# A gated attention kernel on one core: longer rows for the opening weights, four gated chunks per bank, and output rows stored over the gate

## The chip, the cores and the metric

The kernel runs on one core of a Trainium2 chip. The metric is the device time of one execution in microseconds (us). Before the change it was 932.59 us, the median of 3 runs (932.0 to 933.07). The span in a profile is 1.7 to 1.9 us shorter than the device time of the same run. A run's time moves by some 0.5 us and at times more from one execution to the next (nine runs of the kernel before spread over 1.0, 1.4 and 0.6 us in the three sets of the experiments), and this study is about differences of about that size, so the text says each time how many runs a number rests on.

## The reference

```python
xn = layernorm(x)                                   # x: 2048 x 640, bf16
q  = xn @ wq                                        # 32 heads of 192
p  = softmax(q @ k[last 512 keys].T * 192 ** -0.5)
s  = (p @ v[last 512 keys]) @ wo
h  = sigmoid(xn @ w_gate) * (xn @ w_up)             # 1536 features
g  = silu(h @ w_down)
out = x + s * g
```

## The kernel before: the parts that matter here

The kernel has three stages: the gate (the lines of `h` and `g`, up to about 166 us), then eight groups of four heads, and within the last group the final sums and the stores. TensorE does matmuls into four double banks of PSUM (`bank[0..3]`), ScalarE the sigmoids, the exponentials and some copies out of PSUM, VectorE most of the rest; GpSimd has a small part in the sums.

The opening. The rows of the weights are cut into pieces, so that work can start before everything is in. `load_f(w, r, f0, f1)` loads columns `f0*128` to `f1*128` of all 640 rows. Two chunks of 128 bf16 are 512 bytes of a row, four are 1 KB.

```python
load_x(0, 1)                                   # one tile of 128 rows of x, 160 KB
load_f(nc.sync, wg_sb, wg_r, 0, 2)             # 320 KB in rows of 512 B
load_x(1, 1)
load_f(nc.sync, wu_sb, wu_r, 0, 2)
load_x(2, 1)
load_f(nc.sync, wg_sb, wg_r, 2, 4)
load_f(nc.sync, wu_sb, wu_r, 2, 4)
load_x(3, 1)
for f0, f1 in ((4, 8), (8, NF)):               # 640 KB each, rows of 1 KB
    load_f(nc.sync, wg_sb, wg_r, f0, f1)
    load_f(nc.sync, wu_sb, wu_r, f0, f1)
```

The first 512 rows of x are four tiles. Each is normalised on VectorE, turned (transposed) by five matmuls of TensorE, and copied out of PSUM. Only then can its matmuls run. For the first four chunks of features this is done tile by tile, one chunk in one bank at a time: 5 gate matmuls, 5 up matmuls (each 128 x 128 x 128), a sigmoid, a product.

```python
def gated(b, f, r0, r1, k, between=None, amid=None):
    for half, w in ((0, wg_sb), (1, wu_sb)):
        for c in range(NCD):                    # NCD = 5
            nc.tensor.matmul(bank[k][:, half, 0:r1 - r0], lhsT=w[:, c, f * P:(f + 1) * P],
                             rhs=xnT[:, b, c, r0:r1], start=(c == 0), stop=(c == NCD - 1))
        if half == 0 and amid is not None:
            turn_pe(amid)                       # turn the next tile here; ScalarE copies it
    # sigmoid of the gate half on ScalarE, product with the up half on VectorE
# ...
piece(0, 0, lambda: normal(1))                  # piece(tile, chunk, work for VectorE, tile to turn)
piece(0, 1)
piece(0, 2, second_half(2), 1)                  # the turn of tile 1, between gate and up of chunk 2
piece(0, 3)
# ... tiles 1 and 2 alike, tile 3 without a turn; then chunks 4 to 11 with all 512 columns
```

The end. In the last group each finished tile is multiplied by its gate and added to `acc`, which by then holds x plus the gate times the sums of the earlier groups; then it is stored.

```python
fin = tc.tile_pool(name="fin", bufs=4)
# ... in project(u, q, k, out_eng), for the last group:
o_sb = fin.tile([P, D], F32, name="o_sb", bufs=2)
r_sb = fin.tile([P, D], BF16, name="row")       # one of 4 buffers
nc.vector.tensor_tensor(o_sb[:], wide(k)[:, 0:D], gate[:, t, :], ALU.mult)      # the product
nc.vector.tensor_tensor(r_sb[:, d0:d1], o_sb[:, d0:d1], acc[:, t, d0:d1], ALU.add)  # the sum
eng.dma_start(of[t * P:(t + 1) * P, d0:d1], r_sb[:, d0:d1])                     # the store
```

The softmax here doesn't subtract the row's maximum and nothing guards it: scores larger than these inputs give would overflow.

## Time and profile before

| | before |
|---|---|
| time, median of 3 runs | 932.59 us |
| PE (TensorE matmul) busy | 917.8 us of a 931.5 us span (the traced run took 933.39 us) |
| first gated matmul | 6.33 us |
| first weights of the stage with 512 columns (chunk 4) loaded into TensorE | 18.79 us |
| last matmul ends | 925.48 us |
| last sum starts on VectorE | 927.85 us |

First, from the page of the kernel before, the line of the chain that ended last, by engine (shares of the span). The last two entries are the queues of SyncE and VectorE.

```profile
PE 97%; DMA 1%; DVE 1%; issue 1%; SPq 0%; DVEq 0%
```

The chain is 97% TensorE, so only stretches in which TensorE waits, or in which something else ends the program, can be shortened by this change. The table of waits of TensorE, for the kernel before (what waited, what ended the wait; us in total, times, longest) says where it waits. I leave out the wait before its warm-up matmuls.

```profile
PE bank L231 <- DMA wg_sb<-in_B_w_gate_dram: 1.4, 1, 1.4
...
PE bank L231 <- DMA wu_sb<-in_B_w_up_dram: 0.6, 2, 0.4
PE bank L231 <- DVE xnT L216: 0.3, 1, 0.3
```

These few waits are all that the table has, and they lie in the first 10.5 us. The timeline of TensorE's matmuls for the kernel before shows them (start, time from the first start to the last end, line, output<-inputs, shape, count; in brackets the idle time and what ended it).

```profile
6.33 0.44 PE L231 MATMUL bank<-xnT,wg_sb 128*128 128x128 bf16 x5 [0.26 <-DVE xnT L216]
7.03 0.45 PE L231 MATMUL bank<-xnT,wu_sb 128*128 128x128 bf16 x5 [0.26 <-DMA wu_sb<-in_B_w_up_dram]
...
9.41 0.45 PE L231 MATMUL bank<-xnT,wg_sb 128*128 128x128 bf16 x5 [1.37 <-DMA wg_sb<-in_B_w_gate_dram]
9.70 0.44 PE L213 MATMUL bank<-ident,xn 128*128 128x128 bf16 x5
10.51 0.45 PE L231 MATMUL bank<-xnT,wu_sb 128*128 128x128 bf16 x5 [0.37 <-DMA wu_sb<-in_B_w_up_dram]
...
13.59 0.44 PE L231 MATMUL bank<-xnT,wu_sb 128*128 128x128 bf16 x5
13.99 0.44 PE L231 MATMUL bank<-xnT,wg_sb 128*128 128x128 bf16 x5
```

Five matmuls of 128 columns take 0.28 to 0.29 us from start to start (9.41 to 9.70): 56 ns each. TensorE stands still from about 8 us to 9.41 us for the second piece of gate weights, and again before 10.51 us for the second piece of up weights. By then it has done 5 of the 32 groups of five matmuls that the four tiles need. The line at 13.59 followed by 13.99 shows one more thing: 0.12 us of idle before tile 2, as its copy by ScalarE is only just late.

The loads in that time, from the table of stretches of the kernel before (stretch; its length and TensorE's busy time, count; PEld, DVE, ACT, POOL likewise; granted clock; share of the DMA engines; GB/s in the last column):

```profile
5.00:6.00 1.00, 0.94 (x11) 0.59 (x9) 0.88 (x3) 0.99 (x2) 0.00 (x0) 1.00 1.07 288
6.00:7.00 1.00, 0.51 (x6) 0.26 (x4) 0.93 (x4) 0.07 (x1) 0.00 (x0) 1.00 1.02 295
7.00:8.00 1.00, 0.97 (x15) 0.84 (x15) 0.64 (x3) 0.28 (x1) 0.57 (x1) 1.00 1.09 285
```

At the other end, the chain of waits of the kernel before from 914 us on (start, length, what):

```profile
915.74 0.83 DVE o_sb L425
...
916.60 0.82 DVE row L429
...
920.73 3.84 DMA out_dram<-row
...
924.67 0.34 DVE row L429
...
927.00 0.83 DVE o_sb L425
...
927.85 0.56 DVE row L429
```

From 915.74 us VectorE's products (L425) and sums (L429) of 0.82 us each are the chain. At 920.73 us a store begins that is complete only at 924.57 us, and the sum at 924.67 waits for it: its row buffer is the one of that store. The table of waits of VectorE after 895 us has it as one line:

```profile
DVE row L429 <- DMA out_dram<-row: 1.6, 1, 1.6
```

The store of that row could have gone out at about 917.5 us, when its sum ended. It was issued on SyncE behind four transposing transfers that occupied SyncE's queue from 915.41 to 920.62 us.

### The profile page before, as it was taken

What the parts mean: (1) busy time and instruction counts of PE and PEld (TensorE: products, weight loads), DVE (VectorE), ACT (ScalarE), POOL (GpSimd) and SP (SyncE); (2) the same over time, 40 slices, a digit from 0 to 9 for tenths busy, and PEclk for the clock granted to TensorE, in tenths of its full rate; (3) what the DMA queues carried; (4) which work ended last, traced back from release to release, by engine and by line L of the source; (5) the groups of instructions that cost most, each with busy time, mean ns of one, the idle gap of its engine ahead of it and who ended that gap; (6) DMA issues with size and microseconds to landing.
All of it is one profiled execution on the core that took longest, in us unless ns stands there. A gap on an engine that the chain in (4) does not pass through costs nothing.

```text
span 931.5 us, 18073 instructions
## 1 busy us (share of the span) xinstructions
PE 917.8 (99%) x7957; PEld 546.1 (59%) x8037; DVE 469.3 (50%) x749; ACT 306.2 (33%) x341; POOL 126.5 (14%) x154
## 2 busy tenths in 40 slices
PE   8999999999999999999999999999999999999997
PEld 6445455566655566665566666556666666666665
DVE  5552522454554554455455445544555555554667
ACT  4222222433333333333333333333333333333340
POOL 1000010400010002000200020002000205555000
PEclk9999999999999999999999999999999999999999
DMA  9410420616223533433342433253326234422223
GB/s 303 94 22 8 110 63 1 195 36 135 63 52 77 109 80 61 77 85 99 65 77 60 120 68 77 56 124 69 77 51 128 69 72 77 89 63 63 56 70 92
DMA packets 159119, 76.69 MB, mean 82 GB/s; under 512 B 140816, under 2 KB 152960, under 8 KB 159040
## 3 DMA queue, kind: packets, MB, share of 16 engines
q1 hardware_dynamic: 151216, 46.56, 25.4%
q0 software_dynamic: 7248, 28.38, 10.6%
q8 instruction: 63, 1.03, 0.5%
q10 hardware_dynamic: 576, 0.59, 0.2%
q14 instruction: 16, 0.13, 0.0%
HBM read 39.45 MB, written 2.62 MB: 45 GB/s over the span
## 4 chain that ended last, share of the span: by engine, by line
PE 97%; DMA 1%; DVE 1%; issue 1%; SPq 0%; DVEq 0%
PE bank L383 22%; PE bank L420 21%; PE bank L400 19%; PE bank L365 18%; PE bank L231 11%; PE bank L245 6%; DMA wu_sb<-in_B_w_up_dram 1%; PE bank L333 1%; DVE o_sb L425 0%; DMA out_dram<-row 0%; DVE row L429 0%; SPq L149 0%; SPq L154 0%; PE bank L213 0%; DVEq L505 0%
## 5 line engine op out<-in xcount | busy, mean ns | idle before, releaser
L369 ACT ACTIVATE E<-bank 128x1024 bf16<-128x1024 f32 x256 | 257.8, 1023 | 477.3 <-PE bank L365 465.4
L383 PE MATMUL bank<-xnT,wq_sb 64*128 64x512 bf16 x1860 | 231.3, 376 | 0.0
L420 PE MATMUL bank<-wo_sb,oT 128*128 128x128 bf16 (+1 forms) x1473 | 225.2, 296 | 3.3
L365 PE MATMUL bank<-qT,kT 64*128 64x512 bf16 x1536 | 202.1, 376 | 0.0
L400 PE MATMUL bank<-vbuf,E 128*128 128x193 bf16 x2048 | 191.0, 247 | 0.0
L400 PEld LDWEIGHTS <-E 128*128 128x128 bf16 x2048 | 167.8, 98 | 24.2 <-issue 13.6
L390 DVE CAST qT<-bank 128x1024 bf16<-128x1024 f32 x93 | 113.9, 1225 | 132.8 <-PE bank L383 132.8
L420 PEld LDWEIGHTS <-oT 128*128 128x128 bf16 x1536 | 121.3, 98 | 76.6 <-issue 0.4
L383 PEld LDWEIGHTS <-wq_sb 64*128 64x128 bf16 x1860 | 97.0, 100 | 104.8
L365 PEld LDWEIGHTS <-kT 64*128 64x128 bf16 x1536 | 73.0, 94 | 90.0 <-issue 8.8
L406 DVE TENSOR_TENSOR o_st<-bank,rden 128x768 bf16<-128x768 f32 x128 | 122.6, 957 | 5.1 <-DVE rden L405 0.8
L435 DVE TENSOR_TENSOR acc<-bank,acc 128x640 f32<-128x640 f32 x96 | 79.2, 825 | 43.2 <-PE bank L420 43.1
L231 PE MATMUL bank<-xnT,wg_sb 128*128 128x512 bf16 (+1 forms) x296 | 61.4, 336 | 1.8 <-DMA wg_sb<-in_B_w_gate_dram 1.4
L231 PE MATMUL bank<-xnT,wu_sb 128*128 128x512 bf16 (+1 forms) x295 | 61.5, 336 | 0.9 <-DMA wu_sb<-in_B_w_up_dram 0.6
L388 DVE COPY seen<-bank 128x2 f32<-128x2 f32 x93 | 14.8, 159 | 93.7 <-PE bank L383 93.6
L405 DVE RECIPROCAL rden<-bank 128x4 f32<-128x4 f32 x128 | 23.3, 182 | 71.4 <-PE bank L400 71.4
L239 DVE TENSOR_TENSOR hT<-bank,sig 128x512 bf16<-128x512 f32 (+1 forms) x60 | 34.7, 582 | 46.4 <-ACT sig L236 46.4
L236 ACT ACTIVATE sig<-bank 128x512 bf16<-128x512 f32 (+1 forms) x60 | 30.6, 512 | 73.3 <-PE bank L231 68.6
L245 PE MATMUL bank<-wd_sb,hT 128*128 128x128 bf16 (+1 forms) x376 | 52.4, 297 | 0.4
L106 POOL DMA_DIRECT2D vbuf<-in_A_v_cache_dram x28 | 20.9, 747 | 184.9 <-PE bank L400 184.9
L245 PEld LDWEIGHTS <-hT 128*128 128x128 bf16 x384 | 29.7, 98 | 23.1
L231 PEld LDWEIGHTS <-wg_sb 128*128 128x128 bf16 x300 | 26.6, 98 | 27.5 <-DMA wg_sb<-in_B_w_gate_dram 1.5
(44 smaller groups left out, 256.3 us busy)
## 6 DMA issues: line engine op xcount, KB each, us to landing
wo_sb<-in_A_wo_dram POOLq DMA_DIRECT2D x8, 960.0 KB, 7.5
wq_sb<-in_A_wq_dram POOLq DMA_DIRECT2D x7, 960.0 KB, 6.7
k_st<-in_A_k_cache_dram POOLq DMA_DIRECT2D x7, 768.0 KB, 8.2
vbuf<-in_A_v_cache_dram POOLq DMA_DIRECT2D x28, 192.0 KB, 3.0
row<-in_A_x_dram POOLq DMA_DIRECT2D x16, 160.0 KB, 2.6
oT<-o_st SPq DMA_TRANSPOSE x128, 2.6
x_sb<-in_A_x_dram SPq DMA_DIRECT2D x3, 640.0 KB, 11.0
wd_sb<-in_B_w_down_dram SPq DMA_DIRECT2D x1, 1920.0 KB, 14.5
```

The source lines that it names most:

```text
L231: nc.tensor.matmul(bank[k][:, half, 0:r1 - r0], lhsT=w[:, c, f * P:(f + 1) * P], rhs=xnT[:, b, c, r0:r1], start=(c == 0), stop=(c == NCD - 1))
L236: nc.scalar.activation(sig[:, 0:r1 - r0], bank[k][:, 0, 0:r1 - r0], AF.Sigmoid)
L239: nc.vector.tensor_tensor(hT[b][:, f, r0:r1], bank[k][:, 1, 0:r1 - r0], sig[:, 0:r1 - r0], ALU.mult)
L245: nc.tensor.matmul(wide(k)[:, d0:d1], lhsT=hT[b][:, f, q * P:(q + 1) * P], rhs=wd_sb[:, f, d0:d1], start=(f == 0), stop=(f == NF - 1))
L365: nc.tensor.matmul(bank[k][:, i, :], lhsT=kT[r, pr, j, c * P:(c + 1) * P], rhs=q[r, pr * DJ + j, :], start=(j == 0), stop=(j == DJ - 1))
L369: nc.scalar.activation(E[u, pr][:, c, :, :], bank[k][:], AF.Exp, scale=scale_qk)
L383: nc.tensor.matmul(bank[k][:, half, :], lhsT=wq[r, c, col:col + DJ * (P - 1) + 1:DJ], rhs=xnT[r, b, c, :], start=(c == 0 and not second), ...
L390: nc.vector.tensor_copy(qT[u][:, 2 * m:2 * m + 2, :], bank[k][:])
L400: nc.tensor.matmul(o4[:, q, 0:DH + 1], lhsT=e[:, c, h % 2, q * P:(q + 1) * P], rhs=v[:, h, c, 0:DH + 1], start=(c == 0), stop=(c == KC - 1))
L406: nc.vector.tensor_tensor(o_st[u][:, :, h * DH:(h + 1) * DH], o4[:, :, 0:DH], rden[:].to_broadcast([P, TQ, DH]), ALU.mult)
L420: nc.tensor.matmul(wide(k)[:, d0:d1], lhsT=oT[u][:, cc, q * P:(q + 1) * P], rhs=wo[:, cc, d0:d1], start=(cc == 0), stop=(cc == GC - 1))
L435: nc.vector.tensor_tensor(acc[:, t, :], wide(k)[:, 0:D], acc[:, t, :], ALU.add)
```

## The change

The intent: get the first weights in sooner with rows twice as long; use fewer and larger sigmoids and products by putting four chunks of a tile into one bank; get the first tile ready sooner by turning it in two parts; and rid the tail of its wait for a row buffer by writing the row over the gate, which nobody needs any more.

```diff
-        load_f(nc.sync, wg_sb, wg_r, 0, 2)
         load_x(1, 1)
-        load_f(nc.sync, wu_sb, wu_r, 0, 2)
-        load_x(2, 1)
-        load_f(nc.sync, wg_sb, wg_r, 2, 4)
-        load_f(nc.sync, wu_sb, wu_r, 2, 4)
-        load_x(3, 1)
-        for f0, f1 in ((4, 8), (8, NF)):
+        for f0, f1 in ((0, 4), (4, 8), (8, NF)):
             load_f(nc.sync, wg_sb, wg_r, f0, f1)
             load_f(nc.sync, wu_sb, wu_r, f0, f1)
+            if f0 == 0:
+                load_x(2, 1)
+                load_x(3, 1)
 ... (turn_pe takes a range of chunks, a bank and the copying engine; normal takes column ranges;
      the first half of tile 1's statistics moves ahead of tile 0's reciprocal)
+        def tile_gates(t, amid):
+            k = t % 3
+            r = slice(t * P, (t + 1) * P)
+            for half, w in ((0, wg_sb), (1, wu_sb)):
+                for f in range(FT):                      # FT = 4
+                    if (half, f) == (1, 2) and amid is not None:
+                        turn_pe(amid, 0, NCD, bank[3][:, amid % 2, :], nc.scalar)
+                    for c in range(NCD):
+                        nc.tensor.matmul(bank[k][:, half, f * P:(f + 1) * P], ...)
+            # one sigmoid of 512 columns, one product of 512 columns
 ...
-        normal(0)
-        stats_half(1, 0)
-        turn_pe(0)
-        dummy(3)
+        normal(0, ((0, 3 * P), (3 * P, D)))
+        turn_pe(0, 0, 3, bank[3][:, 0, :], nc.vector)
+        turn_pe(0, 3, NCD, bank[2][:, 0, :], nc.scalar)
+        dummy(2)
         stats_half(1, 1)
         stats_end(1)
-        ... (16 pieces, with the statistics and normalisations of VectorE between them)
+        normal(1)
+        full_stats(2)
+        tile_gates(0, 1)
+        normal(2)
+        full_stats(3)
+        tile_gates(1, 2)
+        normal(3)
+        tile_gates(2, 3)
+        tile_gates(3, None)
 ...
-            r_sb = fin.tile([P, D], BF16, name="row")
             nc.vector.tensor_tensor(o_sb[:], wide(k)[:, 0:D], gate[:, t, :], ALU.mult)
+            r_sb = gate[:, t, :]
```

Note a detail of the turn: `(half, f) == (1, 2)` puts it before the third of four up chunks, so 10 matmuls follow it in its tile. Before, 15 followed.

More of the change, by code (lines that the diff above doesn't have):

```diff
@@ L196, in stats_end @@
                 nc.scalar.activation(junk[:], eps_t[:], AF.Sigmoid)
+                stats_half(1, 0)
                 nc.vector.reciprocal(rstd[:], rstd[:])
@@ L201, in stats_end, with normal, turn_pe @@
             ln[t] = mv, rstd
-        def normal(t):
+        def normal(t, parts=((0, D),)):
             mv, rstd = ln[t]
             xn = xpool.tile([P, D], BF16, name="xn")
-            nc.vector.tensor_scalar(xn[:], xt[t], mv[:, 0:1], rstd[:, 0:1],
-                                    op0=ALU.subtract, op1=ALU.mult)
+            for d0, d1 in parts:
+                nc.vector.tensor_scalar(xn[:, d0:d1], xt[t][:, d0:d1], mv[:, 0:1], rstd[:, 0:1],
+                                        op0=ALU.subtract, op1=ALU.mult)
             ln[t] = xn
-        def turn_pe(t):
-            pT = bank[3][:, t % 2, 0:NCD * H2].bitcast(BF16).rearrange("p (c n) -> p c n", c=NCD)
-            for c in range(NCD):
+        def turn_pe(t, c0, c1, bk, eng):
+            pT = bk[:, 0:NCD * H2].bitcast(BF16).rearrange("p (c n) -> p c n", c=NCD)
+            for c in range(c0, c1):
                 nc.tensor.transpose(pT[:, c, :], ln[t][:, c * P:(c + 1) * P], ident[:])
-            dst = xnT[:, 0, :, t * P:(t + 1) * P]
-            if t == 0:
-                nc.vector.tensor_copy(dst, pT)
+            dst = xnT[:, 0, c0:c1, t * P:(t + 1) * P]
+            if eng is nc.vector:
+                nc.vector.tensor_copy(dst, pT[:, c0:c1, :])
             else:
-                nc.scalar.activation(dst, pT, AF.Copy)
+                nc.scalar.activation(dst, pT[:, c0:c1, :], AF.Copy)
         def turn_dma(t):
@@ L224, with gated @@
         hT = {}
-        def gated(b, f, r0, r1, k, between=None, amid=None):
+        def gated(b, f, k, between=None):
+            r0, r1 = 0, TB
             if b not in hT:
@@ L232, in gated @@
                                      rhs=xnT[:, b, c, r0:r1], start=(c == 0), stop=(c == NCD - 1))
-                if half == 0 and amid is not None:
-                    turn_pe(amid)
             sig = bwork.tile([P, TB], BF16, name="sig")
@@ L264, in norm_piece @@
             return step if i <= TQ else None
-        dummy(20)
-        stats_half(0, 0)
-        stats_half(0, 1)
-        stats_end(0)
-        normal(0)
-        stats_half(1, 0)
-        turn_pe(0)
-        dummy(3)
+        FT = 4
+        def tile_gates(t, amid):
+            if 0 not in hT:
+                hT[0] = hpool.tile([P, NF, TB], BF16, name="hT")
+            k = t % 3
[5 more added lines that the diff above has]
+                    for c in range(NCD):
+                        nc.tensor.matmul(bank[k][:, half, f * P:(f + 1) * P],
+                                         lhsT=w[:, c, f * P:(f + 1) * P], rhs=xnT[:, 0, c, r],
+                                         start=(c == 0), stop=(c == NCD - 1))
+            sig = bwork.tile([P, TB], BF16, name="sig")
+            nc.scalar.activation(sig[:], bank[k][:, 0, :], AF.Sigmoid)
+            nc.vector.tensor_tensor(hT[0][:, 0:FT, r],
+                                    bank[k][:, 1, :].rearrange("p (f n) -> p f n", f=FT),
+                                    sig[:].rearrange("p (f n) -> p f n", f=FT), ALU.mult)
@@ L275, with full_stats @@
+        def full_stats(t):
+            stats_half(t, 0)
+            stats_half(t, 1)
+            stats_end(t)
+        dummy(20)
+        full_stats(0)
+        normal(0, ((0, 3 * P), (3 * P, D)))
+        turn_pe(0, 0, 3, bank[3][:, 0, :], nc.vector)
+        turn_pe(0, 3, NCD, bank[2][:, 0, :], nc.scalar)
+        dummy(2)
         stats_half(1, 1)
         stats_end(1)
-        stats_half(2, 0)
-        k = 0
-        def piece(t, f, before=None, amid=None):
-            nonlocal k
-            gated(0, f, t * P, (t + 1) * P, k, before, amid)
-            k = (k + 1) % 3
@@ L285, in second_half @@
-        def second_half(t):
-            return lambda: (stats_half(t, 1), stats_end(t))
-        piece(0, 0, lambda: normal(1))
-        piece(0, 1)
-        piece(0, 2, second_half(2), 1)
-        piece(0, 3)
-        piece(1, 0, lambda: normal(2))
-        piece(1, 1, lambda: stats_half(3, 0))
-        piece(1, 2, second_half(3), 2)
-        piece(1, 3)
-        piece(2, 0, lambda: normal(3))
-        piece(2, 1)
-        piece(2, 2, None, 3)
-        piece(2, 3)
-        for f in range(4):
-            piece(3, f)
@@ L302 @@
-        k = 3
-        for f in range(4, NF):
-            gated(0, f, 0, TB, k, norm_piece(1, f - 4))
+        normal(1)
[7 more added lines that the diff above has]
+        tile_gates(3, None)
+        k = 1
+        for f in range(FT, NF):
+            gated(0, f, k, norm_piece(1, f - FT))
             k = (k + 1) % 4
@@ L307 @@
             for f in range(2):
-                gated(b, f, 0, TB, k)
+                gated(b, f, k)
                 k = (k + 1) % 4
@@ L315 @@
             for f in range(2, NF):
-                gated(b, f, 0, TB, k, norm_piece(b + 1, f - 4) if b + 1 < NB and f >= 4 else None)
+                gated(b, f, k, norm_piece(b + 1, f - 4) if b + 1 < NB and f >= 4 else None)
                 k = (k + 1) % 4
```

## The prediction

> **What bounds the kernel now.** TensorE. The page gives PE 917.8 us busy of a 931.5 us span (99%), and the chain that ended last is 97% PE. PE's waits (the wait table of that engine) after its warm-up all lie before 10.5 us: 1.4 us for gate weights, 0.6 us for up weights, 0.3 us for the first turned tile. From 10.51 to 915.7 us the chain is matmuls with gaps of 0.05 us, so only the two ends can move. The end is VectorE's: from 915.74 us the chain runs through 0.82 us products (L425) and 0.82 us sums (L429), and holds one 1.58 us wait, from 923.1 to 924.67, of a "row" tile for an earlier output DMA.
>
> **The tail (gain, fairly sure).** The row is written into the gate's place, so no buffer has to come free; the build shows the sums waiting for VectorE and GpSimd only. I walk the chain without the wait: that sum ends at 923.95; PE delivers the last two tiles near 923.8 and 925.5 (timeline: 84 matmuls end at 925.48, 1.65 us per tile); the last product starts near 925.7 instead of 927.0. The gain is 1.3 us, not 1.58.
>
> **The opening (about nothing, unsure).** In the stretch table the 512 B rows move 240 to 310 GB/s before 8.5 us, the 1 KB rows about 350 after. The Trainium skill's page "DMA: Bandwidth & Descriptors", section "Why small descriptors are slow (HBM only)", gives each packet a fixed overhead; this trace agrees in direction. The last small weight load was complete at 10.46 us, some 2 us after its 1.80 MB had moved. Now tile 0 cannot start until 0.98 MB are in, nor turn to the up weights until 1.64 MB are: I estimate landings near 6.9 and 9.0 us, at 335 GB/s and the same 2 us lag, against a first gate matmul at 6.33 before. The first tile turned in two parts saves a few tenths that the weights then eat; and its reciprocal now sits behind a 0.48 us statistics instruction.
>
> From the up weights' landing the rest is 40 matmuls of 56 ns per tile and three turns of 0.28 us. A turn now has 10 matmuls behind it, not 15, so 0.56 us cover its ScalarE copy (the next tile started 1.24 us after the turn's start). Estimated idle: 0.4 us per turn, against 0.1 before, plus 0.15 us for tiles 1 and 2, as copy 0.70, sigmoid 0.60, product 0.68 and normalisation 0.45 now follow each other before the next turn. From 9.0 us that is 10.4 us: the 512-column stage starts near 19.4 instead of 19.0. Range -1.0 to +1.2 us.
>
> Fewer, larger sigmoids (16 of 0.28 us become 4 of 0.60) and products save ScalarE and VectorE time off the chain; worth nothing.
>
> **Prediction.** 932.6 - 1.3 + 0.3 = 931.6 us, 930.3 to 932.9. Faster by over 2%: 0.5%; within 2%: 99%; slower: 0.5%.
>
> **What would show it.** No wait of the row sums for an output DMA; last product 1.3 us earlier relative to PE's last matmul; PE's first gated matmul at 6.7 to 7.2, a wait for the up weights until 8.5 to 9.5, and gaps of 0.3 to 0.5 us before tiles 1, 2, 3 (on ScalarE's copy of xnT). The time from the first 512-column matmul to PE's last stays within 0.3 us.
>
> **What would make it wrong.** Longer rows landing much sooner (up weights by 8 us: 1 us faster), the x loads of tiles 2 and 3 landing late behind them (slower), or the output DMAs colliding so that the last transfer, not VectorE, ends the kernel.

## The result, and the profile after

The changed kernel took 932.02 us, the median of 4 runs (931.7 to 932.28), against 932.56 us for 4 runs of the kernel before: ratio 0.9994, 95% interval 0.9977 to 1.0012. Ratios here are the mean time of one kernel's fast runs over that of the other's of the same rounds, so not quite the ratio of the quoted medians.

| | before | after (first trace) |
|---|---|---|
| first gated matmul | 6.33 us | 6.94 us |
| last of the first four chunks' weights complete | 10.46 us | 8.64 us |
| weights of chunk 4 loaded into TensorE | 18.79 us | 18.48 us |
| last sum starts on VectorE | 927.85 us | 926.34 us |
| span of this trace | 931.5 us | 930.2 us |

The same line of the page of the kernel after:

```profile
PE 97%; DVE 1%; DMA 1%; ACT 0%; SPq 0%; issue 0%; DVEq 0%
```

The shares of TensorE, VectorE and DMA are the same to the percent: the bound did not change. The table of TensorE's waits of the kernel after:

```profile
PE bank L278 <- ACT xnT L217: 0.7, 3, 0.2
PE bank L177 <- ACT xnT L217: 0.5, 1, 0.5
PE bank L278 <- DMA wu_sb<-in_B_w_up_dram: 0.5, 1, 0.5
```

The three waits for gate weights, for up weights and for the first tile have become three waits for ScalarE's copy of the next turned tile, one for the copy in front of the warm-up matmuls (L177), and one for the up weights. The matmuls of the kernel after, in the timeline:

```profile
6.94 1.28 PE L278 MATMUL bank<-xnT,wg_sb 128*128 128x128 bf16 x20
8.69 0.73 PE L278 MATMUL bank<-xnT,wu_sb 128*128 128x128 bf16 x10 [0.47 <-DMA wu_sb<-in_B_w_up_dram]
9.25 0.44 PE L212 MATMUL bank<-ident,xn 128*128 128x128 bf16 x5
9.53 0.72 PE L278 MATMUL bank<-xnT,wu_sb 128*128 128x128 bf16 x10
10.49 1.28 PE L278 MATMUL bank<-xnT,wg_sb 128*128 128x128 bf16 x20 [0.23 <-ACT xnT L217]
...
13.39 1.28 PE L278 MATMUL bank<-xnT,wg_sb 128*128 128x128 bf16 x20 [0.23 <-ACT xnT L217]
...
16.30 1.28 PE L278 MATMUL bank<-xnT,wg_sb 128*128 128x128 bf16 x20 [0.23 <-ACT xnT L217]
```

The gate half of tile 0 is one run of 20 matmuls at 6.94 us. Then the up weights, a single transfer of 640 KB, hold TensorE until 8.69 us. From there the tiles are regular: 10 matmuls, the turn (L212), 10 matmuls, a wait, the next tile. From the line at 9.53 with its 10 matmuls of 56 ns to 10.49 there are 0.96 us, so 0.40 us are idle (the bracket says 0.23, since the modelled end of a matmul lies after the start of the next one). From 10.49 to 13.39 and from 13.39 to 16.30 it is the same.

The loads, in the stretches of the kernel after:

```profile
5.00:6.00 1.00, 1.00 (x8) 0.87 (x7) 0.39 (x3) 0.99 (x2) 0.00 (x0) 1.00 1.08 378
6.00:7.00 1.00, 0.53 (x6) 0.29 (x5) 0.96 (x3) 0.42 (x2) 0.00 (x0) 1.00 1.09 356
7.00:8.00 1.00, 1.00 (x21) 1.00 (x19) 0.28 (x2) 0.00 (x0) 0.57 (x1) 1.00 1.09 365
```

The longer rows do move faster: 356 to 378 GB/s against 285 to 295 GB/s in the same three stretches.

The tail, in the chain of waits of the kernel after:

```profile
915.43 0.83 DVE o_sb L431
...
916.36 0.82 DVE gate L436
...
925.50 0.74 DVE o_sb L431
...
926.34 0.56 DVE gate L436
```

The store is gone from the chain; products and sums follow each other to the end. From the first product to the last sum's start it took 926.34 - 915.43 = 10.91 us, against 927.85 - 915.74 = 12.11 us before: 1.20 us less. This one trace would say: tail 1.2 us, opening 0.3 us, 1.3 to 1.5 us in all. The medians say 0.5 us. That gap was the question for the experiments.

### The profile page after: what moved, and what is told of

Read it like the earlier page. It is cut to its first block, busy times and chain, and to the rows that moved or that the text cites. A ratio compares the mean times of both kernels' runs of the same rounds, so it can differ in the third digit from the quotient of the medians.

```text
span 930.2 us, 18111 instructions
## 1 busy us (share of the span) xinstructions
PE 922.3 (99%) x8036; PEld 546.3 (59%) x8036; DVE 467.5 (50%) x738; ACT 304.5 (33%) x330; POOL 126.5 (14%) x154
## 4 chain that ended last, share of the span: by engine, by line
PE 97%; DVE 1%; DMA 1%; ACT 0%; SPq 0%; issue 0%; DVEq 0%
PE bank L390 22%; PE bank L427 21%; PE bank L407 19%; PE bank L372 18%; PE bank L231 10%; PE bank L243 6%; PE bank L278 1%; DMA wu_sb<-in_B_w_up_dram 1%; PE bank L340 1%; DVE gate L436 1%; DVE o_sb L431 1%; ACT xnT L217 0%; PE bank L212 0%; SPq L149 0%; SPq L154 0%
## 5 line engine op out<-in xcount | busy, mean ns | idle before, releaser
L427 PE MATMUL bank<-wo_sb,oT 128*128 128x512 bf16 (+1 forms) x1536 | 228.6, 299 | 0.0
L231 PE MATMUL bank<-xnT,wg_sb 128*128 128x512 bf16 x220 | 54.7, 379 | 0.0
L231 PE MATMUL bank<-xnT,wu_sb 128*128 128x512 bf16 x220 | 54.7, 379 | 0.0
L243 PE MATMUL bank<-wd_sb,hT 128*128 128x512 bf16 (+1 forms) x384 | 52.8, 299 | 0.0
L237 DVE TENSOR_TENSOR hT<-bank,sig 128x512 bf16<-128x512 f32 x44 | 30.3, 689 | 43.7 <-ACT sig L234 43.7
L234 ACT ACTIVATE sig<-bank 128x512 bf16<-128x512 f32 x44 | 26.3, 597 | 68.4 <-PE bank L231 63.8
L231 PEld LDWEIGHTS <-wu_sb 128*128 128x128 bf16 x220 | 21.5, 98 | 26.0
```

Source lines behind the costliest of these rows:

```text
L234: nc.scalar.activation(sig[:, 0:r1 - r0], bank[k][:, 0, 0:r1 - r0], AF.Sigmoid)
L237: nc.vector.tensor_tensor(hT[b][:, f, r0:r1], bank[k][:, 1, 0:r1 - r0], sig[:, 0:r1 - r0], ALU.mult)
L243: nc.tensor.matmul(wide(k)[:, d0:d1], lhsT=hT[b][:, f, q * P:(q + 1) * P], rhs=wd_sb[:, f, d0:d1], start=(f == 0), stop=(f == NF - 1))
L427: nc.tensor.matmul(wide(k)[:, d0:d1], lhsT=oT[u][:, cc, q * P:(q + 1) * P], rhs=wo[:, cc, d0:d1], start=(cc == 0), stop=(cc == GC - 1))
```

## The experiments

All outputs are right. Each kernel was timed in five rounds; the kernel before was run beside it (9 runs for each of the three sets: medians 932.67, 932.76 and 932.73 us). Each has one trace.

The theory to which the experiments led: the tail gains some 1.2 us, and the opening costs some 0.5 us, the first trace of the changed kernel being set against a trace of the kernel before with unusually late loads. Experiment 2 still expected the opening to gain 0.2 to 0.4 us, and had the other as its third view. The rival: the opening gains as the trace shows, and the tail's gain is partly lost again.

### Experiment 1: the tail alone

```diff
 (kernel before)
-            r_sb = fin.tile([P, D], BF16, name="row")
             nc.vector.tensor_tensor(o_sb[:], wide(k)[:, 0:D], gate[:, t, :], ALU.mult)
+            r_sb = gate[:, t, :]
```

> Only the output rows in the gate's place, on the kernel before. Theory (the tail gives nearly all of the gain): the 1.58 us wait of a row sum for an output transfer is gone, the last product starts 1.2 to 1.4 us after its place in the kernel before minus nothing else, the span and the timed median fall by 1.0 to 1.4 us against the kernel before, and the first 512-column gate weights still load near 18.8 us. Rival (the tail gain is lost again in the last output transfers or in the longer semaphore path of the sums, and the 0.5 us of the timed medians is the opening): the median falls by less than 0.4 us.

Measured: 931.5 us (931.13 to 931.72), 1.17 us below the kernel before; ratio 0.9987, interval 0.9975 to 1.0. The tail is worth what was predicted. But one part of the expectation failed in a telling way: the opening, of which not one instruction had changed, brought the weights of chunk 4 into TensorE at 17.81 us, not at 18.79. The chain of waits of this kernel shows why:

```profile
3.74 5.74 DMA wu_sb<-in_B_w_up_dram
...
9.53 2.41 PE bank L231 x40
```

The same transfer of the second piece of up weights, issued at 3.74 us in both traces, was complete at 9.48 us here and at 10.46 us in the trace of the kernel before. The landing of the opening loads varies by a microsecond from run to run, and everything behind it moves along. So a difference of 0.3 us between two single traces of the opening says nothing.

One figure makes the traces comparable all the same. From the load of chunk 4's weights to the first weights of the final block of projections it takes 895.03 to 895.05 us in each of the twelve traces. So what differs between two traced runs lies before or after that stretch.

### Experiment 2: the opening alone

```diff
 (kernel after)
             nc.vector.tensor_tensor(o_sb[:], wide(k)[:, 0:D], gate[:, t, :], ALU.mult)
-            r_sb = gate[:, t, :]
+            r_sb = fin.tile([P, D], BF16, name="row")          # as in the kernel before
```

> The whole change without the rows in the gate's place. Theory: the first 512-column gate weights load near 18.5 us instead of 18.8, the 1.58 us wait in the tail is back, and the timed median falls by 0.2 to 0.4 us. Rival (the opening is where the 0.5 us come from): the median falls by 0.5 us or more. Third view (the opening's gain is only this profile's luck in the landing of the loads): the median is equal or worse.

Measured: 933.62 us (933.05 to 934.6), 0.95 us slower than the kernel before; ratio 1.0011, interval 0.9997 to 1.0024. The third view came true. In this trace the up weights came late, in the line of the chain of waits

```profile
2.14 7.17 DMA wu_sb<-in_B_w_up_dram
```

which ends at 9.31 us instead of 8.64, and chunk 4 came at 19.14 us. With experiment 1 the parts add up only roughly: -1.17 + 0.95 = -0.22 us, against -0.54 and (experiment 5) -0.67 us for the whole.

### Experiment 3: only the loads of the change

```diff
 (kernel before)
 ... the load order and sizes of the change; pieces, turns and VectorE's order as before
```

> The kernel before with only the loads of the change (0.64 MB in 1 KB rows, both x tiles first); its one-chunk pieces and its turns stay. Theory (the up weights' landing sets the opening, and the grouped tile gains nothing on TensorE): the up weights land at 8.4 to 8.8 us; from there 155 matmuls of 56 ns, three turns of 0.28 and three waits of 0.12 us put the first 512-column gate weights at 18.3 to 18.7 us, the same as in the whole change. Rival (the grouping of four chunks is what gains): they load at 18.8 us or later.

Measured: 934.26 us (933.07 to 935.92), 1.59 us slower; ratio 1.0018, interval 1.0005 to 1.003. The weights of chunk 4 came at 18.73 us in its trace, just above the range of the theory, so the number is no clear verdict between the two views. The reason is a third one, in its chain of waits:

```profile
2.70 6.43 DMA x_sb<-in_A_x_dram
...
9.16 0.49 DVE st L185
...
10.05 0.45 PE bank L210 x5
```

In the order of the kernel before, VectorE takes the first half of tile 2's statistics ahead of the normalisation of tile 1. With the loads of the change, tile 2 of x comes in after all the weights, at 9.13 us, so VectorE stands there and the turn of tile 1 comes only at 10.05 us. By this trace the load order of the change needs its new order on VectorE; alone it is a loss. But the traced run (933.18 us) was one of the two shortest, and the other three took 1.1 to 2.7 us more; what happened in those was not traced, so the cause of most of the 1.59 us stays open.

### Experiment 4: the change with rows of 512 bytes

```diff
 (kernel after; only the first four chunks)
-            load_f(nc.sync, wg_sb, wg_r, 0, 4)
-            load_f(nc.sync, wu_sb, wu_r, 0, 4)
+            load_f(nc.sync, wg_sb, wg_r, 0, 2)
+            load_f(nc.sync, wg_sb, wg_r, 2, 4)
+            load_f(nc.sync, wu_sb, wu_r, 0, 2)
+            load_f(nc.sync, wu_sb, wu_r, 2, 4)
```

> The whole change, but the first four chunks of each weight loaded as two transfers of 512 B rows in the same order of bytes. Theory (row length sets the rate): the second half of the up weights lands 0.6 to 1.0 us later than 8.64, at 9.2 to 9.7 us, and the first 512-column stage starts 0.5 to 1.0 us later than 18.5. Rival (the order of the loads, not the row length, is what counts): within 0.2 us of the whole change, or even earlier, because the first up half can land early.

Measured: 931.78 us (931.23 to 932.02), not slower than the change at all; ratio 0.999, interval 0.9978 to 1.0003. The rate did fall as the theory had it, in the table of stretches:

```profile
6.00:7.00 1.00, 0.53 (x7) 0.34 (x6) 0.96 (x3) 0.38 (x1) 0.00 (x0) 1.00 1.19 303
```

303 GB/s in this stretch (306 and 305 in the two around it), against 356 to 378 with rows of 1 KB. And the second piece of up weights was complete only at about 9.17 us. But the first piece was in by then, as the timeline of TensorE shows:

```profile
8.13 0.73 PE L283 MATMUL bank<-xnT,wu_sb 128*128 128x128 bf16 x10
...
9.22 0.73 PE L283 MATMUL bank<-xnT,wu_sb 128*128 128x128 bf16 x10
...
12.13 0.45 PE L217 MATMUL bank<-ident,xn 128*128 128x128 bf16 x5 [0.36 <-DVE xn L210]
```

The up half starts at 8.13 us, not at 8.69, and the turn of tile 1 falls into the wait for the second piece, so its copy costs nothing. Later the turn of tile 2 waits 0.36 us for VectorE, because tile 2 of x, behind slower weights, was late. Chunk 4 came at 18.46 us, where the traces of the change have 18.34 to 19.14. So the length of the rows buys rate, and the size of the transfers that it came with gives the gain away, because in these kernels a consumer waits for a whole transfer. (The edit changes row length and number of transfers together; the two were not tried apart, and this reading rests on the trace.)

### Experiment 5: the change again

No edit.

> The whole change once more, unedited, for five rounds and a second trace of its opening. Theory (tail -1.2 us; opening +0.5 to +1.0 us, with a landing of the up weights that moves by up to 1 us between runs): the median is 0.2 to 0.7 us below the kernel before; the up weights land between 8.6 and 9.4 us and the first 512-column gate weights load 9.8 us after them; the tail is as in the first trace. Rival (the first trace's 0.3 us gain of the opening was the rule): the median is 1.3 us or more below.

Measured: 932.09 us (931.71 to 932.56), 0.67 us below the kernel before; ratio 0.9991, interval 0.9978 to 1.0003. The up weights were complete at 8.74 us and chunk 4 came at 18.57 us, 9.83 us after. The theory holds, the rival falls: the whole change does not gain 1.3 us.

### Experiment 6: six row buffers instead of the gate's place

```diff
 (kernel after)
             nc.vector.tensor_tensor(o_sb[:], wide(k)[:, 0:D], gate[:, t, :], ALU.mult)
-            r_sb = gate[:, t, :]
+            r_sb = fin.tile([P, D], BF16, name="row", bufs=6)
 ... (and the x rows of the group before, which share these buffers, bufs=6)
```

A first version with eight buffers of their own did not fit into the memory.

> The whole change, but the output rows in the row buffer again, with 6 buffers in place of 4. Theory (what the tail gains is the wait, not the place): no wait of a row sum for a transfer, as the seventh row needs a buffer only at about 926 us when the first transfer has been complete since 924.6; the tail is as in the whole change or up to 0.2 us shorter, since the sums need no extra semaphore of GpSimd; the median is within 0.3 us of the whole change. Rival (the place is what counts): it falls back to the kernel before's tail, 1.3 us slower.

Measured: 931.6 us (931.5 to 931.72), 0.49 us below the change of the same set, more than the 0.3 us allowed; ratio to the kernel before 0.9986, interval 0.9973 to 0.9998. What counts is that the wait goes, not where the row lies. And the place has a small price. The timeline of VectorE for this kernel ends:

```profile
925.06 0.82 DVE L432 TENSOR_TENSOR o_sb<-bank,gate 128x640 f32<-128x640 f32 x1
925.92 0.90 DVE L436 TENSOR_TENSOR row<-o_sb,acc 128x384 bf16<-128x384 f32 x2
```

A sum starts 0.86 us after its product (925.06 to 925.92), where the gate's place needs 0.92 us (925.42 to 926.34): the sum now also waits on a semaphore of GpSimd, which had read the gate (so the build of the changed kernel, by the prediction; the trace does not name the engine), and in the chain of the kernel after each sum is preceded by 0.02 us of VectorE's queue and two gaps. From the first product to the last sum's start this is 926.34 - 915.43 = 10.91 us against 925.92 - 915.28 = 10.64 us: 0.27 us. The other 0.2 us of the 0.49 us fit the opening: chunk 4 came at 18.34 us in this trace and at 18.57 us in that of experiment 5.

### Experiment 7: tile 1 turned during the wait for the up weights

```diff
 (kernel after)
+        AT = (0, 2, 2, 2)
-                    if (half, f) == (1, 2) and amid is not None:
+                    if (half, f) == (1, AT[t]) and amid is not None:
```

> The whole change with the turn of tile 1 moved ahead of the up half of tile 0, into the wait for the up weights. Theory: the turn (0.28 us) and the wait for its ScalarE copy (0.40 us) leave the chain, so tile 1 starts 1.1 to 1.2 us after the up weights land instead of 1.8; if the statistics of tile 2 then do not hold tile 1's turn, the 512-column stage starts 9.1 to 9.4 us after the landing instead of 9.8 us, and the median falls 0.3 to 0.7 us below the whole change. Rival (VectorE's chain behind the x load of tile 2 sets the pace): the gain is below 0.2 us and TensorE shows a wait for the normalised tile 2.

Measured: 931.67 us, four of five runs 931.47 to 931.72 and one of 933.66; the median is 0.42 us below the change of the same set. Ratio to the kernel before 0.9991, interval 0.9978 to 1.0005. In the trace the turn runs at 8.26 us, inside the wait, and tile 1 starts at 9.82 us, 1.12 us after the up half of tile 0 began at 8.70, as expected. The turn of tile 2 then starts at 11.76 us, 0.26 us after the ten matmuls ahead of it (10.94 us plus 0.56), so VectorE's chain takes part of the gain. Chunk 4 came at 18.08 us instead of 18.57, some 9.45 us after the up weights (complete at about 8.63 us, as their first load into TensorE, which waited for them, is at 8.69), just outside the expected 9.1 to 9.4. So the waits behind the turns are real cost in the trace, and the turn's position decides them. The timed gain is less sure: the ratio is the same as that of experiment 5, since it counts the run of 933.66 us too.

### Experiment 8: a version from the findings

```diff
 (kernel after)
+        AT = (0, 2, 0, 2)
-                    if (half, f) == (1, 2) and amid is not None:
+                    if (half, f) == (1, AT[t]) and amid is not None:
 ...
-        tile_gates(1, 2)
-        normal(3)
+        tile_gates(1, 2, lambda: normal(3))     # normalise tile 3 ahead of tile 1's product
 ... and the six row buffers of experiment 6
```

> The whole change with 6 row buffers in place of the gate's place, the turns of tiles 1 and 3 ahead of the up halves, and the normalisation of tile 3 ahead of tile 1's product. Theory: the 512-column stage starts 8.6 to 8.9 us after the up weights land (two turns free of waits), and the median is 1.2 to 1.9 us below the kernel before, 0.7 to 1.1 below the whole change. Rival (the loads' landing alone sets the opening): no better than e6_rows6 by more than 0.2 us.

Measured: 930.81 us (930.8 to 931.62), 1.95 us below the kernel before and 1.28 us below the change; ratio 0.9979, interval 0.9967 to 0.9992. It is faster than both kernels, by little. TensorE's timeline:

```profile
8.38 0.45 PE L212 MATMUL bank<-ident,xn 128*128 128x128 bf16 x5 [0.23 <-DVE xn L205]
...
9.79 1.28 PE L279 MATMUL bank<-xnT,wg_sb 128*128 128x128 bf16 x20
...
12.97 1.28 PE L279 MATMUL bank<-xnT,wg_sb 128*128 128x128 bf16 x20 [0.23 <-ACT xnT L217]
14.08 0.44 PE L212 MATMUL bank<-ident,xn 128*128 128x128 bf16 x5
...
17.71 1.24 PE L231 MATMUL bank<-xnT,wg_sb 128*128 128x512 bf16 x5
```

Chunk 4 came at 17.65 us, 9.0 us after the up half of tile 0 began to load into TensorE (8.65 us, right behind the turn and with no wait for the up weights, so when those were complete does not show). The 8.6 to 8.9 us expected from their landing can thus not be checked. At 0.79 us below experiment 6 the rival falls. Against the change the time gained 1.28 us, more than the 0.7 to 1.1 expected; in the traces chunk 4 comes 0.92 us earlier than in experiment 5, and the tail is 0.27 us shorter. Only one wait for a copy is left, before tile 2 at 12.97 us; after the turn at 14.08 us the next 60 matmuls run without a gap.

### Experiments 9 and 10: the two openings behind the same tail

Experiment 9 is the kernel before with `bufs=6` for the rows and nothing else. Experiment 10 is the kernel of experiment 6 again, on the same chip. Only the opening differs.

> The kernel before with 6 row buffers in place of 4 and nothing else: its own opening, the best tail. Set against the next run, which has the same tail and the change's opening. Theory (the change's opening costs about 0.5 us, by what the tail alone and the whole change measured): the median is 1.2 to 1.8 us below the kernel before and 0.2 to 0.8 us below the next run. Rival (the opening is neutral, the earlier differences were the jitter of the loads): within 0.2 us of the next run.

> The whole change with 6 row buffers once more, beside the previous run on the same chip. It measured 1.16 us below the kernel before by the medians. Theory: it repeats within 0.3 us, and is 0.2 to 0.8 us above the previous run, its up weights landing at 8.5 to 9.3 us. Rival: equal to the previous run within 0.2 us, or below it.

Measured: 931.02 us (930.74 to 931.59; ratio to the kernel before 0.9982, interval 0.9968 to 0.9996) for the opening of the kernel before, and 931.61 us (931.53 to 932.27; 0.999, interval 0.9977 to 1.0002) for that of the change. The opening of the change costs 0.59 us by the medians of five runs each. The ranges hardly overlap, but the 95% intervals of the two ratios do, so I call it likely rather than proven by this pair; the difference of experiments 5 and 1 (0.50 us, by their savings of 0.67 and 1.17) and experiment 2 (0.95 us) point the same way. A comparison across sets is coarse, though: experiments 1 and 9 share an opening and their tails differ by 0.27 us in the traces, yet their savings (1.17 and 1.71 us) differ by 0.54.

The pair also shows what the tail's wait was worth alone. Experiment 9 takes 926.14 - 915.50 = 10.64 us from the first product to the last sum's start, 1.47 us less than the 12.11 us of the kernel before. TensorE's last matmuls, in the timelines of experiment 9 and of the kernel after:

```profile
913.67 11.57 PE L420 MATMUL bank<-wo_sb,oT 128*128 128x512 bf16 x82
```

```profile
913.60 11.57 PE L427 MATMUL bank<-wo_sb,oT 128*128 128x512 bf16 x84
```

They end at 925.24 and 925.17 us. In experiment 9 the last product starts at 925.28 us, 0.04 us later: VectorE is level with TensorE. In the kernel after it starts at 925.42 us, 0.25 us later: there VectorE's own chain, longer by its extra wait per sum, sets the end, and not TensorE's last tile.

The traces alone would not have told. Chunk 4's weights came at 18.79, 17.81 and 18.55 us in the three traces of the old opening (before, experiments 1 and 9), and at 18.48, 19.14, 18.57, 18.34 and 18.36 us in five of the new one. The traced run of the kernel before was a long one (933.39 us, the median is 932.6), and so was that of experiment 9 (931.59, the longest of its five). With the fixed middle one can estimate where chunk 4 comes in a run of median length: in the traces of the kernel before and of experiment 5 the device time is 914.60 and 913.54 us more than chunk 4's time, so medians of 932.73 and 932.09 us put it near 18.1 us in the old opening and 18.55 us in the new one. That is an estimate, not a measurement.

## Why the prediction was right

The prediction was 931.6 us with a range of 930.3 to 932.9 and a tail gain of 1.3 us against an opening loss of 0.3 us. Measured were 932.02 and 932.09 us.

- **What bounds the kernel.** Right. The middle did not move: from chunk 4's weights to the first weights of the final block of projections it took 913.52 - 18.48 = 895.04 us after, and 913.83 - 18.79 = 895.04 us before.
- **The tail, -1.3 us.** Right in cause: the wait is gone, and the last product starts 1.27 us earlier relative to TensorE's last matmul (1.52 us after its end before, 0.25 us after). Right in size too: 1.17 us in the timed medians of experiment 1, 1.20 us in the trace. But the size was partly luck, as two errors cancel. TensorE's last tile takes at most 0.11 us of the 1.58 us, not 0.3: with the wait gone and nothing else changed, the tail is 1.47 us shorter (experiment 9), since a product can start 0.04 us after TensorE's last matmul, where the prediction allowed 0.2. And the gate's place costs 0.27 us of that, 0.06 us at each of seven sums, less some 0.03 us at each product that then follows its sum sooner; the prediction did not foresee it, although it names the extra semaphore.
- **The opening, +0.3 us.** Right in sign and, within its range, in size: 0.5 to 0.6 us by two comparisons (experiments 5 and 1, experiments 10 and 9), 0.95 us by experiment 2. The size is luck, for the two times of which it is the difference were both put too late. The steps for the changed kernel were too pessimistic: the up weights were estimated at 9.0 us and came at 8.50 to 9.31 us in the five traces (8.50 to 8.74 in four of them). The gap of 0.4 us per turn was measured as 0.40 us. The additional 0.15 us for tiles 1 and 2 did not appear: a tile took 2.90 us, of which 2.24 us are 40 matmuls, 0.28 the turn and 0.40 the gap. So 9.8 us passed from the up weights to chunk 4, not 10.4 (the 0.15 us for two tiles are half of that difference; the prediction does not itemise the rest), and the first matmul with 512 columns came at 18.53 us in the first trace, not at 19.4. That the total still came out a little too low, and not much too high, lies at the other side: the trace of the kernel before, from which the 19.0 us was taken, showed its opening later than it is in most runs. Experiment 1 shows 18.1 us by the same reading. (In both timelines the first of these matmuls is probably missing, as only four of five are recorded, so both may be some 0.2 us too late.) (The prediction's own 19.4 against 19.0 would be +0.4; it entered +0.3 in the sum.)
- **Fewer, larger sigmoids and products are worth nothing.** Consistent: no wait of TensorE for a sigmoid or a product is among its waits in either kernel. It was not tried alone.
- **The turn in two parts.** Its gain was predicted to be eaten, and the trace agrees: the first gated matmul came at 6.94 us, later than the 6.33 us before. It was not undone alone. The warm-up matmuls stood in front of it, waiting 0.5 us for ScalarE's copy into the other half of their bank; whether this costs anything was not tried either, but the up half waits for its weights behind them anyway.
- **Longer rows move faster.** Right (357 GB/s against 284 over 4 to 8 us), and the Trainium skill's page "DMA: Bandwidth & Descriptors", section "Why small descriptors are slow (HBM only)", gives the direction. Experiment 4 shows that this did not decide the time.

What stays open: why the same loads land up to 1 us earlier or later from run to run; what the long runs of experiment 3 and the one of experiment 7 did (their mean granted clock was 0.997, in the shorter runs of the same kernels 0.998 to 1.0; whether that is cause or consequence was not traced, but in the traces a mean of 0.998, in experiments 2 and 3, goes with the same middle of 895.03 to 895.04 us); and whether the opening's cost is nearer 0.5 or 0.9 us.

## What to carry to other kernels

A consumer that waits for a whole transfer gets nothing of it early, so a larger transfer at a better rate can start its consumer later than two smaller ones; where the start of the work hangs on it, compare landing times, not GB/s. Before believing a difference between two single traces in a stage that waits for loads, look at the same stage in traces of kernels that did not change it: here it moved by 1 us on its own. A buffer wait at the end of a kernel is worth only what the producing engine and the new waits leave of it (of 1.58 us here, 1.47 with two more buffers and 1.20 in the gate's place), so two more buffers can be better than a cleverer place.

## What the Trainium skill lacked or had wrong

- "DMA: Bandwidth & Descriptors", section "Specifications", gives 512 B as the minimum transfer for line rate. Here loads with rows of 512 B moved 305 GB/s from 4 to 8 us (experiment 4), and with rows of 1 KB 357 GB/s in the changed kernel. (Both are rates of all the core's transfers in that stretch.) No page has rates for HBM loads issued from SyncE at these two row lengths.
- No page says how much the landing of a load varies between executions: the same transfer, with the same ones ahead of it, was complete at 9.48, 10.22 and 10.46 us in three traces.
- "TensorE: Matmul & The Clock Gate", section "Back-to-back issue gap", gives for a sustained stream of weight loads and matmuls about 81 ns per matmul at 128 columns and 131 ns at 512, and calls 56 and 216 ns the isolated case. Here a stream in which every matmul has its own weight load ran at 56 ns at 128 columns (20 in 1.11 us, 16.30 to 17.41 us after) and at 216 ns at 512 (five in 1.08 us, 17.71 to 18.79 us in experiment 8).
- "ScalarE: Activation LUTs", section "What ACT_TABLE_LOAD costs", gives 2.66 us for a switch, of which 1.38 us are a drain. In the changed kernel the switch from the square root to the sigmoid took 1.28 us, from 4.54 to 5.82 us, and lay between an activation that ended at 4.51 us and one that began at 5.83 us; no drain of that length shows.
